# Expert stage of an attention, mixture-of-experts and feed-forward kernel: weight low halves, token order, last narrowing and a branch are rearranged

## The chip, the cores and the metric

The kernel runs on one core of a Trainium2 chip. The metric is device time in microseconds (us) of one execution. Before the change it took 735.32 us (median of 3 runs, 734.01 to 735.62).

## The reference

Three stages, all in float32. Attention over 2 batches, 8 heads, 768 positions of 64 (each position sees 4 sinks and a window of 128). Its output, 1536 tokens of 512, goes through a top-1 mixture of 8 experts, and what comes out through a feed-forward layer with a Mish-like activation:

```
e_idx = argmax(x @ w_gate); gate_w = softmax(x @ w_gate)[e_idx]
eom = sigmoid(x @ w_output_gate)[e_idx]
for e in range(8):                       # expert stage
    h = relu(x[mask_e] @ w1[e]);  ye = h @ w2[e]        # w1: 512x1024, w2: 1024x512
    out[mask_e] = gate_w * eom * ye
h = out @ w_in                           # feed-forward, 512x2048
return (h * tanh(softplus(h))) @ w_out   # 2048x512
```

w_in and w_out arrive as float64 and have to be made into float32 on the chip.

## The kernel before

**Stages.** Attention and routing fill about the first 160 us, the expert stage goes from there to about 470 us, the feed-forward from there to the end. The routing writes each token's row, scaled by its gates, to its expert's place in a table in DRAM and counts the tokens of each expert.

**Split operands.** TensorE multiplies in a reduced format (`fp32r`), so every operand of the expert and feed-forward stages is split into a high half (a rounding copy, on ScalarE) and a low half (value minus high half, an elementwise subtraction). A product is high x high, high x low and low x high. `split_w(unit, p)` (L206, L200) does this for weight piece p: 0 to 3 are four pieces of w1, 4 to 7 of w2, each 128x1024 float32 (512 KB), loaded by SP into one of eight buffers `RAW[p]` by `load_w`/`fetch` (L180, L1037). The low half goes to VectorE for even p and to GpSimd for odd p (L203 to L204). `W1` has two sets of pairs that take turns; `W2S` has one.

**Units and tiles.** The expert with the most tokens left over comes last. A unit is an expert; a tile is 192 of its tokens. Seven units have one tile, the last has three: ten tiles, listed in `TILES`. (A branch `If(more > 0)` at L1132 would run extra tiles if an expert had more tokens; it isn't taken on these inputs: the trace has ten tiles.) The first 128 rows of expert 0 are computed apart, ahead of the tiles, in full float32 (`pre_chunk`, L836): two hidden halves of 512, `first` and `second`, with the weight splits of unit 0 between them. The second hidden half's `second` stands at L1056, then its result is copied to `preT` (L1057), then comes the branch, then `preT` and the first tile's x are transposed.

**One tile** (`tile_mm`, L998) has four blocks b. `first(b)`: 16 matmuls of XS with w1 into PSUM `h`; ScalarE copies the low product, VectorE adds (`t`), ScalarE takes the relu as high half of `hs`, VectorE its low half. `second(b)`: 16 matmuls of `hs` with w2 into `Y`. The order is first 0, 1, 2, second 0, first 3, second 1, then `nxt`, second 2, second 3. `nxt` is `split_x` (L980) of the next tile's x: for each of two halves four transposes on TensorE, a high copy on ScalarE and a subtraction on VectorE into `XS`. `put` (L992) takes `Y` out to `yT`, in the next tile. After each step `tick(i)` issues side work by the tables at L1154 to L1156: weight splits and fetches, steps of the narrowing, and id scatters.

**Order.** Inside `manual_schedule` the named engines run in the order of the program text; each engine works its queue strictly in order, with semaphores between engines. Elsewhere a planner orders the instructions. SP only issues DMAs: a load into `RAW[p]` waits in SP's queue until that buffer's low half has been taken.

**Token order.** `posi` holds each token's place in the sorted order. `place_ids` (L950) scatters token numbers by it into `order` in DRAM, 12 indirect DMAs from GpSimd's queue over the tiles; at the start of the last unit GpSimd loads `idx` back from there (L1176). The output rows are scattered by `idx` at the end.

**Narrowing.** w_in's float64 words become float32 by four operations (`narrow_steps`, L213: a scaling and three integer operations). Sixteen pieces of 128x512; ten are done during attention, the last six (10 to 15) in the tiles (`IN_D`), scaled on GpSimd, stored to `wi32` in DRAM, and loaded back into `RAW` in the last unit (`fetch(E, p)`), where their splits follow.

Of the kernel before, what the change touches and what calls it, by code (L numbers as in the profile page):

```python
# [27 lines left out]
E = 8  # L28
# [15 lines left out]
def tile_kernel(  # L44
# [21 lines left out]
    order = dram.tile([NT, 1], I32, name="order")  # L66
# [71 lines left out]
    tokid = const.tile([P, B * NB], I32, name="tokid")  # L138
# [9 lines left out]
    nc.gpsimd.iota(tokid, [[P, B * NB]], base=0, channel_multiplier=1)  # L148
# [284 lines left out]
    col = mid.tile([P, P], F32, name="col")  # L433
    nc.gpsimd.iota(col, [[1, P]], base=0, channel_multiplier=0, allow_small_or_imprecise_dtypes=True)
# [401 lines left out]
    def pre_chunk():  # L836

        hs = [xpre, rs.tile([P, 512], F32, name="preh1")]
        hT = [rs.tile([P, 512], F32, name="prehT0"), xpre]
# [6 lines left out]
        hps, pts = bank2(), bank2()  # L846
        hps, pts = [hps[:, c] for c in range(2)], [pts[:, c] for c in range(2)]
# [41 lines left out]
    steps = rs.tile([P, E, NX], F32, name="steps")  # L889
# [56 lines left out]
    pre_second, pre_hold = pre_chunk()  # L946
    rt_.close()
    prev = []

    def place_ids(i):  # L950
        sc = nc.gpsimd.indirect_dma_start(
            out=order[:, :], out_offset=bass.IndirectOffsetOnAxis(ap=posi[:, i:i + 1], axis=0),
            in_=tokid[:, i:i + 1], in_offset=None,
        )
        for o in prev:
            tc.declare_no_dep(sc.ins, o.ins, reason="each token has its own place")
        prev.append(sc)

    att.close()


# [5 lines left out]
    nrp = moe.enter_context(tc.tile_pool(name="nrp", bufs=2))  # L967
    hb = moe.enter_context(tc.tile_pool(name="hb", bufs=4))
    tb = moe.enter_context(tc.tile_pool(name="tb", bufs=2))
# [10 lines left out]
    def split_x(xr):  # L980
        pt = bank2()
        for t in range(2):
            for d in range(NP):
                nc.tensor.transpose(pt[:, t, d * HW:(d + 1) * HW], xr[:, t, d * P:(d + 1) * P], ident[0:HW, 0:HW])  # L984
            pv_ = pt[:, t, 0:NP * HW].rearrange("p (d c) -> p d c", c=HW)
            xs_ = XS.rearrange("p d s (c t) -> p d s t c", t=2)
            nc.scalar.activation(xs_[:, :, 0, t], pv_, AF.Copy)
            nc.vector.tensor_tensor(xs_[:, :, 1, t], pv_, xs_[:, :, 0, t].bitcast(F32), ALU.subtract)  # L988
# [9 lines left out]
    def tile_mm(w1s, w2s, nxt, tick):  # L998
# [3 lines left out]
        def first(b):  # L1002
# [13 lines left out]
            nc.vector.tensor_tensor(t, hp[:, :, 0:W], t, ALU.add)  # L1016
            nc.scalar.activation(hs[:, :, 0], t, AF.Relu)  # L1017
# [11 lines left out]
        with tc.manual_schedule(engines=WS):  # L1029
            tick(0)  # L1030
            for i, step in enumerate((
                    lambda: first(0), lambda: first(1), lambda: first(2), lambda: second(0), lambda: first(3),
                    lambda: second(1), nxt, lambda: second(2), lambda: second(3))):
                step()
                tick(i + 1)
# [19 lines left out]
    with tc.manual_schedule(engines={ET.PE}):  # L1055
        pre_second(1, 0, 4)  # L1056
    nc.vector.tensor_copy(preT, yps)  # L1057
    more = values(cnti[0:1, 0:1], mybir.ALL_ENGINES, NX)[0]

    def extra_tiles():  # L1060
# [4 lines left out]
        big3 = [xs_.tile([P, NX, E], F32, name=f"b3{c}") for c in range(2)]  # L1065
        ej, sj, lj, rj = [xs_.tile([P, NX], F32, name=f"j{c}") for c in range(4)]
        j7 = xs_.tile([P, NX], F32, name="j7")
        t64_ = xs_.tile([P, E, E], F32, name="t64_")
        exf = xs_.tile([P, NX, 4], F32, name="exf")
# [57 lines left out]
        for p_ in range(4, 8):  # L1127
            split_w(0, p_)
# [11 lines left out]
    unit_at(1)  # L1140
    for p_ in range(4):
        lw_ = fetch(1, p_)
    with tc.manual_schedule(engines={ET.PE, ET.Activation, ET.DVE}):
        pt_ = bank2()
# [3 lines left out]
        split_x(xr0)  # L1148
    for p_ in range(4, 8):
        fetch(1, p_)  # L1150
# [3 lines left out]
    SPL2 = {0: (0, 1), 1: (2,), 2: (3,)}  # L1154
    SPL1 = {4: (0,), 5: (1,), 6: (2,), 8: (3,)}
    IN_D = {t: (NA + t - 1,) for t in range(1, 7)}  # L1156
    assert NA == 10
    for u in range(NA, NA + 2):
        load_in(u, nrm)
    was = [None]  # L1160
    nst = {}
    for t, (u, k_) in enumerate(TILES):
        if t + 1 < NTL:
            u1, k1 = TILES[t + 1]
            if k1 == 0:
                if u1 + 1 < E:
# [11 lines left out]
        def tick(i):  # L1178
            if i == 1 and was[0] is not None:
                put(was[0])  # L1180
            if u and not k_:
                for p_ in SPL2.get(i, ()):
                    split_w(u, 4 + p_)
                    if u + 1 < E:
                        fetch(u + 1, 4 + p_)
            if u + 1 < E:
                for p_ in SPL1.get(i, ()):
                    split_w(u + 1, p_)
                    fetch(u + 2, p_)
            if u == E - 1:  # L1190
                if k_ == 0 and i == 8:
                    for p_ in range(4, 8):
# [225 lines left out]
```

## Time and profile before

| | |
|---|---|
| median of 3 runs | 735.32 us |
| the profiled execution | 742.38 us |
| its span (first to last instruction) | 740.7 us |
| mean granted TensorE clock | 0.908 of full speed |
| busy: TensorE, VectorE, ScalarE, GpSimd | 633.8, 413.6, 419.0, 203.1 us |

The profile is of one execution. A busy TensorE is not TensorE at its peak: its records include half-clock stretches, and matmuls overlap. In a row, `L984` is the kernel's line, `h<-ident,xr` the tiles written and read, `x4` the number of records put together, and `[8.21 <-DVE XS L988]` says that the engine had been idle for 8.21 us and what ended that. PE is TensorE, DVE VectorE, ACT ScalarE, POOL GpSimd, SP the engine that issues most DMAs. Engines that are off the critical path may idle at no cost.

### The profile page before, as it was taken

Reading aid. Unit: us, or ns where it says so; the run is one execution under the profiler, and the core shown is the slowest. Engines: PE = TensorE matmul, PEld = TensorE weight load, DVE = VectorE, ACT = ScalarE, POOL = GpSimd, SP = SyncE. Lnnn points to the kernel's source line nnn. Section 1 sums busy time; section 2 is a strip of 40 time slices with the busy share of each in tenths; the row PEclk is TensorE's granted clock in tenths of the full one; section 3 lists DMA queues with packets and bytes.
Section 4 is the critical chain, followed back from the end, with each engine's and each line's share of the span. In section 5 each row is a group of like instructions: output and inputs, shape, how many; then the busy total and the mean of one; then the engine's idle time right before and its main releaser. Section 6 shows DMA issues by size and latency. Waiting matters only on the chain.

```text
span 740.7 us, 10023 instructions
## 1 busy us (share of the span) xinstructions
PE 633.8 (86%) x3524; PEld 532.0 (72%) x3524; DVE 413.6 (56%) x847; ACT 419.0 (57%) x769; POOL 203.1 (27%) x175
## 2 busy tenths in 40 slices
PE   6998998677875957859655989899999999999996
PEld 4665666443875956859654989788888888888884
DVE  6797889766337476575571442898763221332122
ACT  4776777425335336254360442797788676776663
POOL 3544447526045363472543111000002000020002
PEclk9899989868788889779796999999999999999999
DMA  7888754414755768788985200333301000010001
GB/s 156 198 224 230 227 184 147 137 69 125 248 188 91 221 141 209 177 181 203 114 223 115 101 1 1 114 120 109 113 1 53 5 1 0 1 58 0 1 0 58
DMA packets 67409, 84.15 MB, mean 114 GB/s; under 512 B 43088, under 2 KB 43088, under 8 KB 67344
## 3 DMA queue, kind: packets, MB, share of 16 engines
q1 hardware_dynamic: 64848, 77.05, 40.6%
q0 software_dynamic: 2352, 6.31, 2.4%
q8 instruction: 31, 0.51, 0.3%
q14 instruction: 34, 0.28, 0.1%
q10 hardware_dynamic: 144, 0.00, 0.0%
HBM read 68.40 MB, written 14.95 MB: 113 GB/s over the span
## 4 chain that ended last, share of the span: by engine, by line
PE 28%; issue 27%; DVE 8%; ACT 5%; DMA 4%; POOL 2%; SPq 0%; POOLq 0%; DVEq 0%; ACTq 0%
PE hp L1273 7%; PE acc L1290 6%; PE Y L1024 5%; PE h L1008 4%; PE h L1011 2%; PE Y L1026 2%; DVE wal L204 2%; DMA order<-tokid,posi 2%; DVE wbl L204 2%; DVE wcl L204 1%; DVE t L1016 1%; ACT wch L202 1%; PE h L984 1%; POOL out_dram L1306 1%; DMA raw<-in_moe_w_dram 1%
## 5 line engine op out<-in xcount | busy, mean ns | idle before, releaser
L1024 PE MATMUL Y<-hs,wch 128*128 128x384 f32 x320 | 110.2, 406 | 0.0
L1324 DVE TENSOR_TENSOR fx<-hp,fx 128x512 f32<-128x512 f32 x48 | 30.9, 685 | 113.4 <-ACT fx L1321 113.4
L1306 POOL DMA_INDIRECT out_dram<-nr,idx x12 | 11.6, 964 | 277.2 <-DVE nr L1302 154.0
L1026 PE MATMUL Y<-hs,wcl 128*128 128x192 f32 x320 | 87.0, 272 | 0.0
L1026 PEld LDWEIGHTS Y<-hs,wcl 128*128 128x128 f32 x320 | 70.4, 220 | 0.0
L1024 PEld LDWEIGHTS Y<-hs,wch 128*128 128x128 f32 x320 | 69.9, 218 | 0.0
L1015 ACT ACTIVATE t<-h 128x384 f32<-128x384 f32 x40 | 19.3, 482 | 88.5 <-PE h L1011 88.5
L1315 ACT ACTIVATE fx<-hp,nln 128x512 f32<-128x512 f32 x48 | 33.1, 690 | 60.1 <-PE hp L1273 59.8
L1016 DVE TENSOR_TENSOR t<-h,t 128x384 f32<-128x384 f32 x40 | 22.1, 553 | 80.3 <-ACT t L1015 80.0
L204 POOL TENSOR_TENSOR wcl<-raw,wch 128x1024 fp32r<-128x1024 f32 x16 | 40.6, 2538 | 85.6 <-ACT wch L202 74.1
L984 PE MATMUL h<-ident,xr 96*128 96x96 f32 x80 | 13.4, 304 | 57.7 <-DVE XS L988 57.6
L568 POOL TENSOR_TENSOR p<-p,sm 128x512 f32<-128x512 f32 (+1 forms) x48 | 46.9, 1005 | 43.7 <-DVE sm L561 24.6
L556 ACT ACTIVATE p<-ms,nm 128x272 f32<-128x272 f32 (+1 forms) x96 | 47.2, 495 | 17.0 <-DVE nm L554 16.4
L984 PEld LDWEIGHTS h<-ident,xr 96*128 96x128 f32 x80 | 9.6, 172 | 59.8 <-DVE XS L988 59.6
L1017 ACT ACTIVATE hs<-t 128x384 fp32r<-128x384 f32 x40 | 21.0, 525 | 43.8 <-DVE t L1016 43.8
L554 DVE CUSTOM_DVE_ANT_0 ms<-s,m 128x272 f32<-128x272 f32 (+1 forms) x96 | 36.5, 407 | 16.2 <-PE s L298 15.9
L1008 PE MATMUL h<-XS,wbh 128*128 128x384 f32 x192 | 44.0, 351 | 0.0
L1018 DVE SCALAR_TENSOR_TENSOR hs<-t,hs 128x384 fp32r<-128x384 f32 x40 | 28.2, 706 | 23.6 <-ACT hs L1017 23.6
L1273 PE MATMUL hp<-yh,wah 128*128 128x512 f32 x96 | 38.3, 399 | 2.1 <-ACT yh L1223 2.1
L1332 DVE TENSOR_TENSOR gl<-fx,gh 128x512 fp32r<-128x512 f32 x48 | 31.5, 689 | 13.6 <-ACT gh L1328 6.2
L222 DVE SCALAR_TENSOR_TENSOR nt<-nr,nt 128x512 int32<-128x512 int32 x32 | 38.7, 1208 | 0.6
L1273 PE MATMUL hp<-yh,wal 128*128 128x512 f32 x96 | 37.9, 395 | 0.0
(275 smaller groups left out, 1749.2 us busy)
## 6 DMA issues: line engine op xcount, KB each, us to landing
raw<-in_moe_w_dram SPq DMA_DIRECT2D x64, 512.0 KB, 6.7
nr<-in_moe_w_in_dram SPq DMA_DIRECT2D x16, 512.0 KB, 6.1
nr<-in_moe_w_out_dram SPq DMA_DIRECT2D x16, 512.0 KB, 3.7
table<-zer SPq DMA_DIRECT2D x17, 256.0 KB, 5.2
wi<-nt SPq DMA_DIRECT2D x16, 256.0 KB, 3.7
raw<-wi SPq DMA_DIRECT2D x8, 512.0 KB, 10.6
xr<-table SPq DMA_DIRECT2D x10, 384.0 KB, 8.1
vr<-in_v_dram SPq DMA_DIRECT2D x16, 192.0 KB, 3.3
```

Of the source, the lines that this page charges most:

```text
L204: eng.tensor_tensor(lo, src, hi.bitcast(F32), ALU.subtract)
L222: lambda: v_.scalar_tensor_tensor(di, hi_, -2147483648, di, ALU.bitwise_and, ALU.bitwise_or),
L554: nc.vector.tensor_tensor_reduce(ms[:, 0:w], s[j][:, 0:w], m, 1.0, 3.0e38, ALU.add, ALU.min, nm[:, j, i:i + 1])
L556: nc.scalar.activation(p[:, j, i, o:o + w], ms[:, 0:w], AF.Exp, bias=nm[:, j, i:i + 1], scale=-1.0, accum_out=sm[:, j, i:i + 1])
L568: nc.gpsimd.tensor_tensor(pb, pb, sm[:, :, i:i + 1].unsqueeze(3).to_broadcast([P, 2, 2 - s0, P]), ALU.mult)
L1008: nc.tensor.matmul(hp[:, f, 0:2 * W], lhsT=w1s[d][0][:, c], rhs=XS[:, d].rearrange("p s c -> p (s c)"), start=(d == 0), stop=False, skip_g ...
L1024: nc.tensor.matmul(Y[:, c, 0:2 * W], lhsT=wh, rhs=hT[b][:, f].rearrange("p s c -> p (s c)"), start=(b == 0 and f == 0), stop=False, skip_g ...
L1026: nc.tensor.matmul(Y[:, c, 0:W], lhsT=wl, rhs=hT[b][:, f, 0], start=False, stop=(b == 3 and f == 1), skip_group_check=True)
L1273: nc.tensor.matmul(h, lhsT=wt[:, (fb % 8) * P:(fb % 8 + 1) * P], rhs=xx[d], start=(k_ == 0), stop=(k_ == 11))
L1290: nc.tensor.matmul(accs[w][tb], lhsT=g_[:, tb * P:(tb + 1) * P], rhs=w_[:, c], start=(fb == 0 and k_ == 0), stop=(fb == NF - 1 and k_ == 2))
L1315: nc.scalar.activation(x_, st[n]["h"], AF.Sigmoid, bias=nln2)
L1332: nc.vector.tensor_tensor(gl, st[n]["x"], st[n]["gh"].bitcast(F32), ALU.subtract)
```

## The change

- Inside the tiles every weight low half goes to VectorE. The ten tiles have 80 steps (`slot`, eight per tile), and a list `jobs` gives each step at most one weight piece: ScalarE takes its high half in that step, VectorE its low half in the next (`low`), and the fetch of the same piece of the next unit is issued right behind.
- `slot` calls stand inside `first` (between the `t` sum and the relu) and at other places of the tile; `split_x` does all eight transposes first, then both high copies, then both subtractions.
- The pieces 10 to 15 of w_in are narrowed on VectorE in the ninth tile, straight into `RAW[5]` to `RAW[7]`; only pieces 8 and 9 and the first half come from `wi32`.
- The id scatters, `order` and its load go. In the ninth tile VectorE makes one-hots of the places, in the tenth TensorE multiplies them (12 small bf16 matmuls) into the ids, which go to `idx`.
- `pre_chunk` is cut in two: the branch `If(more > 0)` stands after the first part; the second part (`rest`) follows it. Fetches of unit 1's first four pieces stand ahead of `rest`. Register values for unit 2 are loaded there too.
- Buffers: `hs` 3 instead of 4, `t` 3 instead of 2; `preh`, `prehT` in a pool of their own.

```diff
@@ pre_chunk @@
             first(1, 0, 2)
-            turn(hT[0], hs[0], pts[0])
+            turn(hT[0], hs[0], bank2()[:, 0])
             for p_ in range(2, 4):
                 split_w(0, p_)
             first(1, 2, 4)
             relu(1)
+
+        def rest():
             second(0, 0, 2)
             split_w(0, 4)
-            hold = turn(hT[1], hs[1], pts[1])
+            turn(hT[1], hs[1], bank2()[:, 0])
             for p_ in range(5, 8):
                 split_w(0, p_)
             second(0, 2, 4)
-        return second, hold
+            second(1, 0, 4)
+
+        return rest
@@ split_x @@
-            nc.scalar.activation(xs_[:, :, 0, t], pv_, AF.Copy)
-            nc.vector.tensor_tensor(xs_[:, :, 1, t], pv_, xs_[:, :, 0, t].bitcast(F32), ALU.subtract)
+        for t in range(2):
+            nc.scalar.activation(xs_[:, :, 0, t], pv_[t], AF.Copy)
+        for t in range(2):
+            nc.vector.tensor_tensor(xs_[:, :, 1, t], pv_[t], xs_[:, :, 0, t].bitcast(F32), ALU.subtract)
@@ tile_mm @@
             nc.vector.tensor_tensor(t, hp[:, :, 0:W], t, ALU.add)
+            slot(i)
             nc.scalar.activation(hs[:, :, 0], t, AF.Relu)
...
         with tc.manual_schedule(engines=WS):
-            tick(0)
...
+            slot(0)
+            first(0, 1)
+            first(1, 2)
+            first(2, 3)
+            second(0)
+            slot(4)
+            first(3, 5)
+            second(1)
+            slot(6)
+            nxt()
+            second(2)
+            slot(7)
+            second(3)
@@ ahead of the tiles @@
     xr0 = load_x(P)
-    with tc.manual_schedule(engines={ET.PE}):
-        pre_second(1, 0, 4)
-    nc.vector.tensor_copy(preT, yps)
     more = values(cnti[0:1, 0:1], mybir.ALL_ENGINES, NX)[0]
...
     unit_at(1)
+    unit_at(2)
     for p_ in range(4):
-        lw_ = fetch(1, p_)
+        fetch(1, p_)
+    with tc.manual_schedule(engines={ET.PE, ET.Activation}):
+        pre_rest()
+    for p_ in range(4, 8):
+        fetch(1, p_)
     with tc.manual_schedule(engines={ET.PE, ET.Activation, ET.DVE}):
+        nc.vector.tensor_copy(preT, yps)
+        split_x(xr0)
...
+    for t, (u, k_) in enumerate(TILES):
+        if u < E - 1:
+            own = [(u, p_) for p_ in (5, 6, 7)] if u else [None] * 3
+            jobs += own + [(u + 1, p_) for p_ in (0, 1, 2, 3, 4)]
+        elif k_ == 0:
+            jobs += [(u, p_) for p_ in (5, 6, 7)] + [(E, p_) for p_ in range(4)] + [None]
+        elif k_ < LT_ - 1:
+            jobs += [("n", x_) for x_ in range(NA, 16)] + [None] * 2
+        else:
+            jobs += [None] * 4 + [(E, p_) for p_ in (4, 6, 5, 7)]
+    def low():
+        while waits:
+            u, p_ = waits.pop(0)
+            hi, lo = wpair(u, p_)
+            nc.vector.tensor_tensor(lo, RAW[p_], hi.bitcast(F32), ALU.subtract)
+            if u + 1 < E or u + 1 == E and p_ <= 4:
+                fetch(u + 1, p_)
+    def job(j):
+        if j is not None and j[0] != "n":
+            nc.scalar.activation(wpair(*j)[0], RAW[j[1]], AF.Copy)
+        low()
+        if j is not None and j[0] == "n":
+            r0, c0 = in_piece(j[1])
+            for x_ in narrow_steps(RAW[4 + r0 // P][:, c0 - 1024:c0 - 512], nrm[j[1] % 2], scale_dve):
+                x_()
+            load_in(j[1] + 2, nrm)
+        elif j is not None:
+            waits.append(j)
+    def hot_of_places():
+        c12 = col[:, 0:NTB]
+        v_.tensor_scalar(pos2[:, 0], posi, P - 1, None, ALU.bitwise_and)
+        v_.tensor_scalar(pos2[:, 1], posi, 7, None, ALU.logical_shift_right)
+        v_.tensor_copy(posf2, pos2)
+        v_.tensor_tensor(hot, col.unsqueeze(1).to_broadcast([P, NTB, P]),
+                         posf2[:, 0].unsqueeze(2).to_broadcast([P, NTB, P]), ALU.is_equal)
...
+    def ids_of_places():
+        ps = bank2()
+        for a in range(NTB):
+            nc.tensor.matmul(ps[:, 0, 0:2 * NTB], lhsT=hot[:, a], rhs=blk[:, a].rearrange("p s m -> p (s m)"),
+                             start=(a == 0), stop=(a == NTB - 1))
+        nc.scalar.activation(ids, ps[:, 0, 0:2 * NTB].rearrange("p (s m) -> p s m", s=2), AF.Copy)
+        v_.scalar_tensor_tensor(ids[:, 0], ids[:, 1], float(P), ids[:, 0], ALU.mult, ALU.add)
+        v_.tensor_copy(idx, ids[:, 0])
@@ loop over the tiles @@
-            nc.gpsimd.dma_start(out=idx, in_=order.rearrange("(i p) o -> p (i o)", p=P))
+            for x_ in range(NA, NA + 2):
+                load_in(x_, nrm)
+        def slot(i):
+            if i == 0 and was[0] is not None:
+                put(was[0])
+            job(jobs[8 * t + i])
+            if t == NTL - 2 and i == 6:
+                hot_of_places()
+        tile_mm(W1[u % 2], W2S, (lambda: split_x(xr1)) if t + 1 < NTL else ids_of_places, slot)
...
     with tc.manual_schedule(engines={ET.Activation, ET.DVE}):
         put(was[0], range(NP + 1))
+        low()
```

## Rows read from the trace of the kernel before

**Rows 1.** The page's busy tenths of TensorE in 40 slices of the span

```profile
PE   6998998677875957859655989899999999999996
```

**Rows 2.** A middle tile on TensorE: start us, us, line, operation, [idle before it <-releaser]

```profile
276.51 0.88 PE L1008 MATMUL h<-XS,wbh 128*128 128x384 f32 x4
...
283.42 0.36 PE L1024 MATMUL Y<-hs,wch 128*128 128x384 f32 x1
...
285.69 0.90 PE L1008 MATMUL h<-XS,wbh 128*128 128x384 f32 x4
...
290.27 0.50 PE L984 MATMUL h<-ident,xr 96*128 96x96 f32 x4
298.98 0.90 PE L984 MATMUL h<-ident,xr 96*128 96x96 f32 x4 [8.21 <-DVE XS L988]
```

**Rows 3.** Waits of all engines from 210 to 390 us: total us, times, longest

```profile
PE h L984 <- DVE XS L988: 53.4, 7, 8.2
```

**Rows 4.** The same tile on VectorE

```profile
283.27 1.23 DVE L204 TENSOR_TENSOR wcl<-raw,wch 128x1024 fp32r<-128x1024 f32 x1 [0.39 <-DMA xr<-table]
...
285.56 0.56 DVE L1018 SCALAR_TENSOR_TENSOR hs<-t,hs 128x384 fp32r<-128x384 f32 x1 [0.59 <-ACT hs L1017]
...
295.43 3.03 DVE L204 TENSOR_TENSOR wal<-raw,wah 128x1024 fp32r<-128x1024 f32 x1 [0.27 <-ACT wah L202]
```

**Rows 5.** The same tile on GpSimd

```profile
294.53 2.85 POOL L204 TENSOR_TENSOR wal<-raw,wah 128x1024 fp32r<-128x1024 f32 x1 [3.13 <-ACT wah L202]
```

**Rows 6.** The same tile on ScalarE

```profile
279.06 0.49 ACT L1015 ACTIVATE t<-h 128x384 f32<-128x384 f32 x1 [6.61 <-PE h L1011]
...
285.43 1.04 ACT L202 ACTIVATE wch<-raw 128x1024 fp32r<-128x1024 f32 x1
```

**Rows 7.** 2 us windows: busy us (xcount) by engine, granted clock, DMA share, GB/s

```profile
186.00:188.00 2.00, 0.90 (x4) 0.61 (x4) 0.47 (x2) 0.51 (x1) 0.00 (x0) 0.50 1.01 391
282.00:284.00 2.00, 2.00 (x18) 2.00 (x16) 1.29 (x2) 1.62 (x3) 0.00 (x0) 1.00 1.00 247
300.00:302.00 2.00, 2.00 (x9) 2.00 (x9) 1.51 (x2) 1.38 (x2) 2.00 (x2) 0.50 0.88 358
```

**Rows 8.** TensorE at the stage's start, first and eighth tile, and feed-forward start

```profile
176.82 3.60 PE L859 MATMUL Y<-raw,xpre 128*128 128x512 f32 x8
...
183.68 0.63 PE L1146 MATMUL h<-ident,preT 128*128 128x128 f32 x4 [3.27 <-DVEq L1132]
...
188.44 1.62 PE L1008 MATMUL h<-XS,wah 128*128 128x384 f32 x4 [1.28 <-DVE XS L988]
...
205.19 0.49 PE L984 MATMUL h<-ident,xr 96*128 96x96 f32 x4
...
405.83 0.53 PE L1011 MATMUL h<-XS,wbl 128*128 128x192 f32 x1 [8.73 <-POOL wbl L204]
...
420.47 0.49 PE L984 MATMUL h<-ident,xr 96*128 96x96 f32 x4
...
470.00 0.50 PE L1273 MATMUL hp<-yh,wah 128*128 128x512 f32 x1 [1.75 <-ACT yh L1223]
```

**Rows 9.** GpSimd beside these stretches

```profile
173.99 2.45 POOL L204 TENSOR_TENSOR wal<-raw,wah 128x1024 fp32r<-128x1024 f32 x1 [2.98 <-ACT wah L202]
176.98 6.05 POOL L204 TENSOR_TENSOR wcl<-raw,wch 128x1024 fp32r<-128x1024 f32 x2 [0.53 <-ACT wch L202]
...
402.31 1.09 POOL L1176 DMA_DIRECT2D idx<-order  x1 [10.16 <-DMA order<-tokid,posi]
```

**Rows 10.** VectorE on 48 elements, and narrowing alone later

```profile
157.07 0.21 DVE L341 TENSOR_TENSOR dl<-L,mx 128x48 f32<-128x48 f32 x1
...
475.18 0.42 DVE L226 TENSOR_SCALAR nt<-nr 128x512 f32<-128x512 f32 x1
...
477.43 0.68 DVE L1264 TENSOR_TENSOR wbl<-nt,wbh 128x512 fp32r<-128x512 f32 x1
```

**Rows 11.** The line that loads w_in pieces: time to landing

```profile
DMA to landing us min/median/max: 4.1/6.1/7.6
```

More of the change, by code (lines that the diff above doesn't have):

```diff
@@ L137, in tile_kernel @@
     ones = mid.tile([P, P], BF16, name="ones")
-    tokid = const.tile([P, B * NB], I32, name="tokid")
+    col = const.tile([P, P], F32, name="col")
+    part = const.tile([P, 1], F32, name="part")
     nc.gpsimd.iota(w8, [[-1, E]], base=E, channel_multiplier=0, allow_small_or_imprecise_dtypes=True)
@@ L147, in tile_kernel @@
     nc.gpsimd.affine_select(upper, ones, [[1, P]], ALU.is_gt, 0.0, base=0, channel_multiplier=-1)
-    nc.gpsimd.iota(tokid, [[P, B * NB]], base=0, channel_multiplier=1)
+    nc.gpsimd.iota(part, [[0, 1]], base=0, channel_multiplier=1, allow_small_or_imprecise_dtypes=True)
+    nc.gpsimd.iota(col, [[1, P]], base=0, channel_multiplier=0, allow_small_or_imprecise_dtypes=True)
     base = [ecap, const.tile([P, E], F32, name="base1")]
@@ L836, in pre_chunk @@
     def pre_chunk():
-        hs = [xpre, rs.tile([P, 512], F32, name="preh1")]
-        hT = [rs.tile([P, 512], F32, name="prehT0"), xpre]
+        hs = [xpre, preh]
+        hT = [prehT, xpre]
         def turn(dst, src, pt):
@@ L844, in turn @@
             return nc.scalar.activation(dst, pt, AF.Copy)
-        hps, pts = bank2(), bank2()
-        hps, pts = [hps[:, c] for c in range(2)], [pts[:, c] for c in range(2)]
+        hps = bank2()
+        hps = [hps[:, c] for c in range(2)]
         def first(hf, a, z):
@@ L945, in tile_kernel @@
     nc.vector.tensor_copy(posi, posf)
-    pre_second, pre_hold = pre_chunk()
     rt_.close()
[L948 to L957, printed above, removed]
     att.close()
+    prp = ExitStack()
+    prp_ = prp.enter_context(tc.tile_pool(name="prp", bufs=1, side="right"))
+    preh, prehT = [prp_.tile([P, DM], F32, name=nm) for nm in ("preh1", "prehT0")]
+    pre_rest = pre_chunk()
     W1[1] = pairs4(ctx.enter_context(tc.tile_pool(name="wp1", bufs=1)), "wb")
@@ L1068, in extra_tiles @@
         t64_ = xs_.tile([P, E, E], F32, name="t64_")
+        big3 = [xs_.tile([P, NX, E], F32, name="b30"), t64_[:, 0:NX]]
         exf = xs_.tile([P, NX, 4], F32, name="exf")
@@ L1147, in tile_kernel @@
         nc.scalar.activation(yT[:, :, 0:P], pt_[:, 0].rearrange("p (d t) -> p d t", t=P), AF.Copy)
-        split_x(xr0)
-    for p_ in range(4, 8):
-        fetch(1, p_)
     TILES = [(u, 0) for u in range(E - 1)] + [(E - 1, k_) for k_ in range(LT_)]
     NTL = len(TILES)
[L1154 to L1159, printed above, removed]
+    jobs = []
@@ new lines, in tile_kernel @@
+    for t, (u, k_) in enumerate(TILES):
[8 more added lines that the diff above has]
+            jobs += [None] * 4 + [(E, p_) for p_ in (4, 6, 5, 7)]
+    assert len(jobs) == 8 * NTL and NA == 10
@@ new lines, in tile_kernel @@
+    jobs.append(None)
+    waits = []
+    def low():
[16 more added lines that the diff above has]
+            waits.append(j)
@@ new lines, in tile_kernel @@
+    hot = xp.tile([P, B * NB, P], BF16, name="hot")
+    blk = xp.tile([P, B * NB, 2, B * NB], BF16, name="blk")
+    pos2 = xp.tile([P, 2, B * NB], I32, name="pos2")
+    posf2 = xp.tile([P, 2, B * NB], F32, name="posf2")
+    ids = xp.tile([P, 2, B * NB], F32, name="ids")
+    NTB = B * NB
+    def hot_of_places():
[5 more added lines that the diff above has]
+                         posf2[:, 0].unsqueeze(2).to_broadcast([P, NTB, P]), ALU.is_equal)
+        v_.tensor_tensor(blk[:, :, 0], c12.unsqueeze(1).to_broadcast([P, NTB, NTB]),
+                         posf2[:, 1].unsqueeze(2).to_broadcast([P, NTB, NTB]), ALU.is_equal)
+        v_.tensor_tensor(blk[:, :, 1], blk[:, :, 0], c12.unsqueeze(2).to_broadcast([P, NTB, NTB]), ALU.mult)
+        v_.tensor_scalar(blk[:, :, 0], blk[:, :, 0], part, None, ALU.mult)
@@ L1165, in tile_kernel @@
             if k1 == 0:
-                if u1 + 1 < E:
+                if u1 + 1 < E and u1 > 1:
                     unit_at(u1 + 1)
```

56 lines of the change are left out of this document (7 added, 49 removed).

## The prediction, made before the changed kernel ran

> **What bounds the kernel now.** I read the page first: in the expert stage TensorE's digits drop again and again, while over the last third, the feed-forward stage, they stay at nine [rows 1]. So the stage that the change touches has slack and the one it leaves alone has none. Then one middle tile on TensorE, which has eight blocks of matmuls and eight transposes to do per tile: after the first four transposes of the next x it stands still for 8.21 us until VectorE has written `XS` [rows 2]. Over the waits between 210 and 390 us that is the largest of TensorE: seven times, 53.4 us [rows 3]. Then the other engines in the same tile. VectorE is late because, just ahead of that subtraction in its queue, a weight low half takes 3.03 us; the same operation takes 1.23 us earlier in the tile [rows 4], in a window in which GpSimd does nothing [rows 7]. The slow one starts at 295.43, and GpSimd's own low half runs from 294.53 to 297.38 [rows 5]: VectorE ends 1.08 us after GpSimd does. So the tile is paced by two engines that hold each other up over low halves, and then by four transposes that wait for the first `XS` subtraction. Once more, in the eighth tile, TensorE waits 8.73 us for a GpSimd low half [rows 8]; that one was queued behind the `idx` load, for which GpSimd had waited 10.16 us until the last id scatter landed [rows 9].
>
> **Lows on VectorE, one per step; transposes together.** TensorE's demand at full clock: four `first` and two `second` blocks, 276.51 to 290.27, 13.76 us; a `second` block is 283.42 to 285.69, 2.27 us, and two are left, 4.54 us; eight transposes, two records of 0.50 us, 1.0 us [rows 2]. Sum 19.3 us. VectorE per tile: eight lows of 1.23, and twelve small operations (four `t` sums, four `hs` lows, two `XS`, two `yT`), all taken at the 0.56 of the `hs` low: 9.84 + 6.72 = 16.6 us [rows 4]. ScalarE: eight high halves of 1.04 and twelve small operations of about 0.5, 14.3 us [rows 6]. Both are under 19.3. In order: a `t` sum stands behind at most one low, so the bank of a block is free about 1.3 us after its matmuls end and wanted again one block (2.29 us) later; the `XS` subtractions end some 1.8 us after the transposes, and two `second` blocks (4.54 us) cover them, now that all eight transposes go first. Three `hs` buffers instead of four suffice: the fourth `hs` is written after `second(0)`. I find no wait of TensorE left over, with about 1 us to spare at the tightest place, the first block's `t` sum behind the two `yT` sums and a low. Weights: SP's queue now holds for each piece a wait for its low and then its fetch, in the order of the lows, and the piece is wanted one tile later, so each has some 17 us. Bytes per tile: eight pieces of 512 KB and 384 KB of x, 4.6 MB in 19.3 us, 238 GB/s; windows with a full DMA share show 247 to 391 GB/s [rows 7]. So a tile costs 19.3 us. From the first tile's transposes to the eighth's are now 420.47 - 205.19 = 215.3 us [rows 8]; seven tiles will take 135.1. Gain 80.2 us, the `idx` wait included, since with the scatters gone GpSimd has nothing queued. The granted clock should stay up too: after its 8 us of idling TensorE is at 0.50 (1.2 GHz) [rows 7]; that loss is part of the 215.3.
>
> The Trainium skill ("SBUF — State Buffer", Who interferes with whom) says that a VectorE operation with two SBUF inputs and a GpSimd operation that reads SBUF lock each other out for a whole instruction, and that DMA never slows an engine. The tile agrees: 297.38 plus one uncontended low gives the end seen. By that rule every low goes to 1.23 us; if DMA writes slowed VectorE, lows would stay at 3.03, which is a rival below.
>
> **The last narrowing, in SBUF.** Six pieces move into tile nine, steps 0 to 5, all four operations of each on VectorE, and their loads start at tile eight, behind its predecessor's fetches on SP. Four operations take 477.43 - 475.18 = 2.25 us where nothing disturbs them [rows 10]; six pieces, 13.5 us. The tile's small operations are 6.7 us. The one-hots of the places: 1536 elements by the slope between 48 (0.21 us [rows 10]) and 1024 (1.23 us [rows 4]), 1.0 ns each, 1.8 us; three operations on 144 at 0.31 and three tiny ones at 0.2, 1.5 us. Sum 23.5 us: here VectorE is the bound. Piece 12 waits for a load issued when piece 10 is done (two buffers); queued behind it on VectorE are the `hs` low and the `t` sum, for which TensorE waits. A load lands 4.1 to 7.6 us after issue [rows 11]; in between VectorE has 3.4 us of work (piece 11 and two block operations). At 4.1, as the weight loads are gone by then, I add 1 us per pair, twice: 25.5 us; at 7.6 it is 31. The fourth `hs` low and the one-hots come late, TensorE waits some 3 us before its last `second` block and again before tile ten, and I charge tile ten 1.6 us of half clock (a middle tile that starts at 298.98 is at 0.50 to at least 302 [rows 2, 7], 3 us or a little more, of which half is lost).
>
> By the Trainium skill ("SBUF — State Buffer", The DMA setup-cost knee) a 512 KB load is estimated at 2 us plus 1.2 us. The row has 4.1 as the least; by the page's figure tile nine would take 24 us. I keep the row.
>
> Tile ten: 19.3 less the transposes' 1.0, plus twelve small bf16 matmuls in their place (0.6; 0.3 to 2), plus 1.6: 20.5 us. Its high halves and lows have steps 4 to 7; the last low stands after the last `yT` sum and delays only low halves of y, which the feed-forward's first eight matmuls cover; without that cover it costs 1.2 us. From tile eight's transposes to the feed-forward: 1.0 + 4.5 + 25.5 + 20.5 + 1.7 (the wait for `yh` [rows 8]) = 53.2 us, now 470.00 - 420.47 = 49.5. Loss 3.7 us. The six stores and three reloads of `wi32` that go were hidden.
>
> **The branch moved up.** Now all engines resume together at 183.68; GpSimd's last low ends at 183.03 [rows 8, 9]. With the branch ahead of the second part of the shared chunk's work (`rest`), only low 3 is before it on GpSimd, which ends at 176.44 [rows 9]; they resume near 177.1. TensorE will have stood since about 173 (176.82 less one hidden half of 3.60 [rows 8] and four transposes), so it starts at half clock. It still has two hidden halves of 3.60 us and four transposes, 7.6 us, then x's transposes and `XS`, 2.6 us: first matmul at 187.3 at full clock, 195 at half, against 188.44 [rows 8]. In return the first tile then runs at full clock: 13.8 us to the transposes instead of 205.19 - 188.44 = 16.75. They come at 201 to 209; I take 205, no change, 4 us either way. SP's fetches of unit 1 start 6 us earlier, behind unit 2's register loads; the piece is wanted 20 us later. The moved `col` and the new `part` are short GpSimd work at the start, beside the first loads: nothing.
>
> **Sum.** 80.2 - 3.7 + 0 = 76.5 us. The profiled execution took 742.4 us (span 740.7), so 665.9; the median shown, 735.3, is 7 us below that execution, and so 658.8. I say 659 us.
>
> **Rivals.** (1) TensorE keeps short waits in each tile: one low (1.23 us) too late at two places, 2.4 us, seven times, gives 676. For it: three engines in tight order with 1 us of slack. Against: the transposes no longer wait for one another. (2) DMA bound: a tile before moved 8 x 512 + 384 + 512 + 256 KB, 5.4 MB, in (215.3 - 8.7) / 7 = 29.5 us, 182 GB/s. If that is the ceiling of this mix, 4.6 MB take 25.2 us, 5.9 more seven times: 700. Against: 391 GB/s at the stage's start [rows 7]. (3) The other side: lows stay long on VectorE although GpSimd is idle, because DMA writes hold it up. At 3.03 us a tile has 8 x 3.03 + 6.7 = 30.9 us of VectorE, seven make 216.6, and with the 3.7 behind them 740; it turns slower from 2.94 us per low. At 3.6 (1.23 plus a wait of 2.4, the length of a GpSimd low [rows 9]) it is 35.5 us per tile, 772. Against: the 1.23 us low ran while the DMA share was 1.00 [rows 4, 7]. (4) It doesn't do what it says: the planner leaves part of the moved work where TensorE waits for it; half the gain, 697.
>
> **Chances.** Forecast 0.76; (1) 0.10; (2) 0.05; (3) 0.02, slower; (4) 0.05; others 0.02, half of them slower. The forecast's own range: tile nine 2 shorter or 6 longer, start 4 either way, tiles 19.0 to 20: 651 to 674. The 8-in-10 range takes in (1): 647 to 679. Faster by over 0.2% (what a measurement of this kernel can tell from no change) 0.96, within it 0.01, slower 0.03.
>
> **What would show it.** Right: eight weight lows per tile on VectorE near 1.23 us, no GpSimd work in the stage, tiles 19 to 20 us apart with the clock at 1.00, one longer tile (24 to 28 us) with VectorE busy throughout, feed-forward starting near 393 us. Wrong: TensorE still waiting for `XS`, lows over 2 us, ScalarE waiting for `raw` to land, or a first tile that starts after 196 us.

## The result, and the profile after

The changed kernel takes 666.3 us (median of 4 runs, 664.71 to 667.05) against 735.47 before (4 runs): 0.906 of the time, interval 0.9032 to 0.9081. The forecast was 659 us, its range 647 to 679. The profiled execution has a span of 665.3 us against 740.7.

TensorE's busy tenths and granted clock, from the page after; the digits of before are in [rows 1].

```profile
PE   6988999877599999999998979999999999999996
...
PEclk9999888968799999999998979999999999999999
```

Counting slices from 1, the dips of the expert stage are gone but for three: slice 11, the branch at its start, and the small ones in slices 22 and 24, tile nine and the stage's end. TensorE's waits in the stage, 205 to 395 us (line, releaser, total, times, longest), answer to [rows 3]:

```profile
PE hp L1309 <- ACT yh L1259: 4.9, 1, 4.9
PE Y L1018 <- DVE hs L1012: 2.8, 2, 2.6
PE h L1001 <- DVE t L1009: 0.5, 1, 0.5
```

All three lie in tile nine or later. The lows on VectorE, 205 to 335 us, grouped by line and shape (count, busy us and mean ns, then idle time before them), against the 1.23 and 3.03 us of [rows 4]:

```profile
L1173 DVE TENSOR_TENSOR wcl<-raw,wch 128x1024 fp32r<-128x1024 f32 x28 | 34.0, 1214 | 0.0
L1173 DVE TENSOR_TENSOR wal<-raw,wah 128x1024 fp32r<-128x1024 f32 x14 | 17.0, 1216 | 0.0
L1173 DVE TENSOR_TENSOR wbl<-raw,wbh 128x1024 fp32r<-128x1024 f32 x13 | 15.8, 1216 | 0.0
```

The stage on TensorE in order of time (start, duration, what it waited for), against [rows 2, 8]:

```profile
175.01 3.75 PE L858 MATMUL Y<-raw,prehT 128*128 128x512 f32 x4 [7.32 <-DVEq L1128]
...
201.44 0.83 PE L975 MATMUL h<-ident,xr 96*128 96x96 f32 x8
...
258.58 0.83 PE L975 MATMUL h<-ident,xr 96*128 96x96 f32 x8
...
334.76 0.83 PE L975 MATMUL h<-ident,xr 96*128 96x96 f32 x8
...
360.68 0.69 PE L1018 MATMUL Y<-hs,wch 128*128 128x384 f32 x1 [2.62 <-DVE hs L1012]
...
365.06 1.53 PE L1001 MATMUL h<-XS,wbh 128*128 128x384 f32 x4
...
389.87 0.79 PE L1309 MATMUL hp<-yh,wah 128*128 128x512 f32 x1 [4.93 <-ACT yh L1259]
```

Read the transposes (L975) as a clock: 201.44, 258.58 three tiles later, 334.76 four more tiles later, 19.05 us a tile throughout. Cutting both executions at the same places: up to the first tile's transposes 205.19 before, 201.44 after (-3.75 us); seven tiles 215.28 and 133.32 (-81.96); from there to the feed-forward 49.53 and 55.11 (+5.58); the feed-forward to the end 270.7 and 275.4 (+4.7). Together -75.4, the difference of the spans. The medians differ by 69.2 only: the profiled execution of before took 742.38 us, and its start was a late one, as the second look below shows.

### The profile page after: what moved, and what is told of

It is laid out like the page before. It is cut to its first block, busy times and chain, and to the rows that moved or that the text cites. A ratio compares the mean times of both kernels' runs of the same rounds, so it can differ in the third digit from the quotient of the medians.

```text
span 665.3 us, 9962 instructions
## 1 busy us (share of the span) xinstructions
PE 614.8 (92%) x3536; PEld 511.9 (77%) x3536; DVE 410.0 (62%) x892; ACT 418.6 (63%) x770; POOL 102.3 (15%) x126
## 4 chain that ended last, share of the span: by engine, by line
PE 41%; issue 26%; DVE 2%; POOL 2%; DMA 1%; ACT 0%; POOLq 0%; ACTq 0%
PE Y L1018 9%; PE hp L1309 8%; PE h L1001 8%; PE acc L1326 6%; PE h L1004 5%; PE Y L1020 4%; DMA nr<-in_moe_w_in_dram 1%; POOL out_dram L1342 1%; POOL wcl L205 1%; PE h L975 1%; DVE raw L222 0%; DVE raw L223 0%; ACT t L988 0%; DVE yT L989 0%; DVE raw L221 0%
## 5 line engine op out<-in xcount | busy, mean ns | idle before, releaser
L1018 PE MATMUL Y<-hs,wch 128*128 128x384 f32 x320 | 96.8, 367 | 2.8 <-DVE hs L1012 2.8
L1020 PE MATMUL Y<-hs,wcl 128*128 128x192 f32 x320 | 81.6, 255 | 0.0
L1018 PEld LDWEIGHTS Y<-hs,wch 128*128 128x128 f32 x320 | 61.2, 191 | 3.2 <-DVE hs L1012 3.2
L1020 PEld LDWEIGHTS Y<-hs,wcl 128*128 128x128 f32 x320 | 62.2, 194 | 0.0
L555 ACT ACTIVATE p<-ms,nm 128x272 f32<-128x272 f32 (+1 forms) x96 | 47.3, 495 | 17.5 <-DVE nm L553 17.4
L1008 ACT ACTIVATE t<-h 128x384 f32<-128x384 f32 x40 | 19.6, 490 | 29.4 <-PE h L1004 29.4
L1326 PE MATMUL acc<-wdh,gh 128*128 128x512 f32 x96 | 37.8, 394 | 0.0
L1326 PE MATMUL acc<-wdl,gh 128*128 128x512 f32 x96 | 37.6, 392 | 0.0
L1173 DVE TENSOR_TENSOR wcl<-raw,wch 128x1024 fp32r<-128x1024 f32 x30 | 36.4, 1214 | 0.0
L988 ACT ACTIVATE t<-Y 128x384 f32<-128x384 f32 (+1 forms) x22 | 10.2, 463 | 39.8 <-PE Y L1020 32.9
L299 PE MATMUL s<-kh,qh 64*128 64x272 f32 (+1 forms) x96 | 24.8, 420 | 9.3 <-DVE nm L553 9.3
L604 ACT ACTIVATE ph<-pt 128x512 f32<-128x512 f32 (+1 forms) x48 | 25.9, 557 | 10.5 <-PE pt L296 10.5
```

The costliest lines, as they stand in the source:

```text
L555: nc.scalar.activation(p[:, j, i, o:o + w], ms[:, 0:w], AF.Exp, bias=nm[:, j, i:i + 1], scale=-1.0, accum_out=sm[:, j, i:i + 1])
L1018: nc.tensor.matmul(Y[:, c, 0:2 * W], lhsT=wh, rhs=hT[b][:, f].rearrange("p s c -> p (s c)"), start=(b == 0 and f == 0), stop=False, skip_g ...
L1020: nc.tensor.matmul(Y[:, c, 0:W], lhsT=wl, rhs=hT[b][:, f, 0], start=False, stop=(b == 3 and f == 1), skip_group_check=True)
L1173: nc.vector.tensor_tensor(lo, RAW[p_], hi.bitcast(F32), ALU.subtract)
L1326: nc.tensor.matmul(accs[w][tb], lhsT=g_[:, tb * P:(tb + 1) * P], rhs=w_[:, c], start=(fb == 0 and k_ == 0), stop=(fb == NF - 1 and k_ == 2))
```

## The experiments

All ran beside the kernel before, whose median was 735.7 to 736.0 us on these chips. Ratios are against that median; the changed kernel's own is 0.9057 (0.9032 to 0.9081). "Seven tiles" is the time from the first tile's transposes to the eighth's. "The chunk" is the work on the first 128 rows of expert 0, ahead of the tiles.

**Odd lows back on GpSimd** (in the changed kernel):

```diff
-            nc.vector.tensor_tensor(lo, RAW[p_], hi.bitcast(F32), ALU.subtract)
+            (nc.gpsimd if p_ % 2 else nc.vector).tensor_tensor(lo, RAW[p_], ...)
```

> The changed kernel, but the low halves of odd pieces go to GpSimd again, one per step. Theory (VectorE and GpSimd hold each other up): VectorE lows that start while GpSimd works take 2 to 3 us again, the t and hs operations slip behind them, and TensorE, which has about 1 us of slack per tile, waits 0.5 to 2.5 us in each of seven tiles: 670 to 685 us. Rival (GpSimd was only slow by itself, and spreading one low per step hides it): lows on VectorE stay at 1.22 us, tiles stay 19.05 us apart, 664 to 669 us.

670.38 us, ratio 0.913 (0.9088 to 0.9172); seven tiles 138.0 us. VectorE and then GpSimd in one tile:

```profile
217.97 1.22 DVE L1173 TENSOR_TENSOR wal<-raw,wah 128x1024 fp32r<-128x1024 f32 x1
221.78 3.43 DVE L1173 TENSOR_TENSOR wal<-raw,wah 128x1024 fp32r<-128x1024 f32 x1
```

```profile
218.49 5.64 POOL L1173 TENSOR_TENSOR wal<-raw,wah 128x1024 fp32r<-128x1024 f32 x2 [3.61 <-ACT wah L1179]
```

The hold-up is there: the low that meets GpSimd's takes 3.43 us instead of 1.22. But it costs only 4.7 us over seven tiles, the low end of what the theory gave: in this order TensorE wants little at once of what stands behind a long low (between 200 and 340 us its longest wait for `XS` is 1.0 us).

**x's halves in turn again** (in the changed kernel): `split_x` as it was, four transposes, copy, subtraction, twice.

```diff
-        for t in range(2):
-            nc.scalar.activation(xs_[:, :, 0, t], pv_[t], AF.Copy)
-        for t in range(2):
-            nc.vector.tensor_tensor(xs_[:, :, 1, t], pv_[t], ...)
+            nc.scalar.activation(xs_[:, :, 0, t], pv_, AF.Copy)
+            nc.vector.tensor_tensor(xs_[:, :, 1, t], pv_, ...)
```

> The changed kernel, but x is turned half by half as before (four transposes, high copy, subtraction, then the next four). Theory: the second four transposes wait for the first subtraction, which stands behind a low in VectorE's queue: about 1.8 us of TensorE per tile, nine times, 16 us: 679 to 686 us, granted clock still 1.00 in the tiles. Rival (with short lows VectorE is early enough, so the order of the transposes carries nothing): 665 to 669 us.

692.84 us, ratio 0.943 (0.9385 to 0.9472), more than the theory's 679 to 686. The second four transposes wait 1.81 us in every tile, as expected, and in tile nine much longer, behind the narrowing:

```profile
205.76 0.55 PE L976 MATMUL h<-ident,xr 96*128 96x96 f32 x4 [1.81 <-DVE XS L979]
...
387.23 0.90 PE L976 MATMUL h<-ident,xr 96*128 96x96 f32 x4 [8.77 <-DVE XS L979]
```

Seven tiles take 150.7 us (+17.4), and tile eight's transposes to the feed-forward 64.1 (+9.0): the two add up to the 26 us. The clock was not 1.00 throughout, as the theory had it: behind two of the seven waits it fell (0.57 from 228 to 230 us), and those tiles took 22.7 us instead of 21.1.

**`rest` ahead of the branch** (in the changed kernel):

```diff
     pre_rest = pre_chunk()
+    with tc.manual_schedule(engines={ET.PE, ET.Activation}):
+        pre_rest()
...
-    with tc.manual_schedule(engines={ET.PE, ET.Activation}):
-        pre_rest()
```

> The changed kernel, but the second part of the shared rows' work stands ahead of the branch again. Theory: TensorE works through instead of standing 7.3 us at 167.7, but stands later, between that work and the first tile, until GpSimd's lows of pieces 5 and 7 end; the first tile starts at about 186 to 189 us as before and runs its first blocks at half clock, 3 us lost: 667 to 673 us. Rival (the move is worth the whole early wait): 673 to 680 us. Rival (the move costs its wait, and undoing it helps): 660 to 664 us.

661.6 us, ratio 0.902 (0.8965 to 0.9079), which the time alone doesn't tell from 0.9057. The chunk's first matmul and the first tile's transposes, in the changed kernel:

```profile
163.56 1.98 PE L850 MATMUL h<-raw,preT 128*128 128x512 f32 x4 [0.53 <-ACT xpre L287]
...
201.44 0.83 PE L975 MATMUL h<-ident,xr 96*128 96x96 f32 x8
```

and with `rest` ahead of the branch:

```profile
162.20 1.98 PE L850 MATMUL h<-raw,preT 128*128 128x512 f32 x4 [0.53 <-ACT xpre L287]
...
177.77 0.85 PE L977 MATMUL h<-ident,xr 96*128 96x96 f32 x8 [1.78 <-SPq L1130]
...
180.95 0.41 PE L1003 MATMUL h<-XS,wah 128*128 128x384 f32 x1 [1.89 <-ACT yT L1150]
...
196.36 0.83 PE L977 MATMUL h<-ident,xr 96*128 96x96 f32 x8
```

The first tile's transposes come 5.1 us earlier, but 1.4 us of this were there before the branch: the chunk itself began earlier, and over all traces it begins anywhere between 159.0 and 167.1 us. Counted from the chunk, the transposes come after 34.2 us instead of 37.9. So moving the branch up cost 3.7 us: with `rest` ahead, TensorE fills the time in which it now stands 7.32 us for the branch. Both theories that called the move a gain fall; the rival that undoing it helps holds.

**All lows on VectorE** (alone, in the kernel before):

```diff
-        eng = eng or (nc.vector if p % 2 == 0 else nc.gpsimd)
+        eng = eng or nc.vector
```

> The kernel before, with all weight low halves on VectorE and nothing else changed (old tables of steps, id scatters and narrowing in place). Theory (the mutual hold-up of VectorE and GpSimd is the largest part of the gain): lows fall to about 1.22 us, tiles go from 29 to 21 to 24 us, the 8.7 us wait in the eighth tile goes as nothing stands behind the idx load: 675 to 700 us. Rival (VectorE becomes the bound, as the lows stand in bunches ahead of the subtraction): tiles stay at 27 to 30 us, 715 to 740 us.

728.15 us, ratio 0.990 (0.9877 to 0.9929). Waits of TensorE, 200 to 425 us, and VectorE ahead of one late `XS`:

```profile
PE h L984 <- DVE XS L988: 46.1, 8, 7.3
```

```profile
267.92 1.23 DVE L204 TENSOR_TENSOR wbl<-raw,wbh 128x1024 fp32r<-128x1024 f32 x1 [0.39 <-ACT wbh L202]
269.06 0.42 DVE L220 TENSOR_SCALAR nt<-nt 128x512 int32<-128x512 int32 x1
...
270.12 1.22 DVE L204 TENSOR_TENSOR wbl<-raw,wbh 128x1024 fp32r<-128x1024 f32 x1
271.26 0.55 DVE L988 TENSOR_TENSOR XS<-h,XS 128x384 fp32r<-128x384 f32 x1
```

Every low is short, and the `XS` wait only falls from 8.2 to 7.3 us. VectorE is now late because the old tables put lows and narrowing steps in a bunch ahead of `XS`. Still the seven tiles fall to 195.8 us, by 19.5. The total hides that, because the edit reaches further than the change: unit 0's lows, ahead of the tiles, go to VectorE too (the change leaves them split), and the first transposes come 46.7 us after the chunk's first matmul instead of 37.1 (second look below).

**The transposes together** (alone, in the kernel before), and then **together with all lows on VectorE**: the new `split_x`; and that with the line above.

> The kernel before with one part of the change alone: the eight transposes of x together, then both copies, then both subtractions; the weight lows stay split between VectorE and GpSimd, in their old places. Theory A (the wait for the first XS is the cost, whoever else is late): 53.4 us of waits go, and the half clock behind them, -50 to -65, 670 to 685 us. Theory B (lows and XS come late as well, and are only waited for in another place, in the next tile's first block): -15 to -35, 700 to 720, and TensorE waits for XS or a low ahead of a first block. Other side: slower, if the two subtractions now stand together behind a long low and the next first block needs both.

> The kernel before with two parts of the change: the transposes together and every low on VectorE; the planner still places the splits, and the id scatters and the idx load stay. If these two parts are all that the seven tiles need: tiles of about 19 us but for tile eight, and about 735 less 73, 660 to 668. If the fixed places (one high half and one low per step, between t and relu) carry a part: 675 to 700, with VectorE and ScalarE working in bunches between the transposes, as they did with the lows alone on VectorE. By e11 and e4 the two would add up if independent.

The first: 716.87 us, ratio 0.974 (0.9712 to 0.9768), seven tiles 201.2. Its waits of TensorE, 205 to 405 us:

```profile
PE h L1013 <- POOL wbl L204: 20.3, 4, 12.3
PE h L1010 <- DVE XS L990: 16.9, 6, 2.9
PE h L1013 <- POOL wal L204: 8.8, 3, 3.3
```

That is theory B: the 8.2 us waits are gone, and TensorE waits in the next tile's first block instead, for `XS` and for a GpSimd low. The second: 688.75 us, ratio 0.936 (0.933 to 0.9392), seven tiles 162.7. Waits, 205 to 395 us:

```profile
PE h L1010 <- DVE XS L990: 13.9, 6, 2.3
PE Y L1026 <- DVE hs L1020: 3.0, 6, 1.0
PE h L984 <- DMA xr<-table: 2.1, 1, 2.1
```

The same edit to the lows lengthens the start here too. The first transposes come 49.1 us after the chunk; TensorE's wait at the branch is, here and then in the second look at the kernel before:

```profile
PE h L1148 <- DVEq L1134: 13.6, 1, 13.6
```

```profile
PE h L1146 <- DVEq L1132: 4.4, 1, 4.4
```

GpSimd, rid of its lows, now runs six id scatters ahead of that branch (163.10 to 173.89 us); whether they are what it waits for isn't shown.

In the tiles, this is what follows a wait for `XS` (2 us windows: busy us by engine, granted clock, DMA share, GB/s):

```profile
331.00:333.00 2.00, 1.29 (x4) 1.32 (x5) 2.00 (x4) 0.00 (x0) 0.00 (x0) 0.71 0.97 324
333.00:335.00 2.00, 2.00 (x9) 2.00 (x9) 1.43 (x2) 0.00 (x0) 0.00 (x0) 0.50 0.99 286
```

A wait of 2.3 us for `XS` is paid almost twice: the matmuls behind it run at 0.50 for some 3.4 us (331.7 to 335.1), of which half is lost. Lined up, the seven tiles take 215.3 us; 195.8 with the lows moved; 201.2 with the transposes together; 162.7 with both; 133.3 with the fixed places as well. No part carries the gain alone: the two together save 52.6 us where each alone saves 19.5 and 14.1, and the last 29.4 come with the rest of the rewritten order (one high half and one low per step, the low between the `t` sum and relu, the narrowing and the id scatters out of these tiles). How these share the 29.4 us was not tested. In the wait shown, ScalarE's copies of x already start late, at 328.97, behind three high halves, while the transposes stand at 323.37; the two narrowing steps ahead of VectorE's subtraction take 1.1 us.

**The idx load at the last tile** (in the kernel before):

```diff
-        if t == E - 1:
+        if t == NTL - 1:
             nc.gpsimd.dma_start(out=idx, ...)
```

> The kernel before, with the idx load issued at the last tile instead of ahead of tile eight, so that GpSimd doesn't stand before it while the id scatters land; the scatters stay. Theory (the 8.73 us wait of TensorE in tile eight is all that the scatters cost): the wait goes, GpSimd's low halves of that tile are ready on time, -8 to -11 us with the half clock behind it, about 726. Rival (the scatters themselves delay GpSimd's lows in other places): more than 12 us can't come from this edit alone, and the wait only moves to the last tile: 733 to 736.

735.84 us, ratio 0.999 (0.9962 to 1.0018), and no finding on the load: the planner put it in the same place, and all instructions of GpSimd and SP stand in the order of before. What the id scatters cost was therefore not measured. The run is a second look at the kernel before:

```profile
161.99 1.98 PE L851 MATMUL h<-raw,preT 128*128 128x512 f32 x4 [0.53 <-ACT xpre L286]
...
199.10 0.49 PE L984 MATMUL h<-ident,xr 96*128 96x96 f32 x4
```

Seven tiles take 213.6 us, then 47.9 and 270.3. The profiled execution of before had thus come to its tiles some 6 us late: its chunk began at 167.09, 5.1 us later than here, and its first four matmuls took 3.78 us instead of 1.98. Counted from the chunk, the first transposes come after 37.1 us here and 38.1 there, against 37.9 in the changed kernel: the start as a whole is within 1 us of what it was, where the spans alone showed 3.75 us gained. The seven tiles' saving is 80 to 82 us by either.

**32 bytes more among the constants** (in the changed kernel):

```diff
-    part = const.tile([P, 1], F32, name="part")
+    part = const.tile([P, 16], F32, name="part")[:, 0:1]
```

> The changed kernel with 32 bytes more in its constants, so that the weights, XS and the hidden buffers stand in SBUF where they stood before the change (224 instead of 192 modulo 512 bytes); nothing else differs. Theory (place of the matmul operands): the feed-forward's groups of 12 matmuls of 512 columns go from 2.80 and 2.76 us back to 2.72, the stage from 275.4 to about 271 us, the total to about 661.5 us (-4.7). Rival (the 4.7 us come from something else, such as the state in which the stage begins, or from one execution to the next): groups stay at 2.76 to 2.80, total at 666 within 1.

660.95 us, ratio 0.897 (0.8952 to 0.8997). Matmuls of the feed-forward, 475 to 735 us, by line (count, busy us, mean ns), first the changed kernel and then with the 32 bytes:

```profile
L1309 PE MATMUL hp<-yh,wah 128*128 128x512 f32 x60 | 23.7, 396 | 0.0
...
L1309 PE MATMUL hp<-yh,wch 128*128 128x512 f32 x32 | 12.7, 398 | 0.0
```

```profile
L1309 PE MATMUL hp<-yh,wah 128*128 128x512 f32 x60 | 23.3, 389 | 0.0
...
L1309 PE MATMUL hp<-yh,wch 128*128 128x512 f32 x32 | 12.5, 389 | 0.0
```

The mean falls from 396 to 398 ns to 389, and the starts of successive matmuls stand 0.227 us apart instead of 0.233 at the same clock of 1.00. The feed-forward takes 270.1 us instead of 275.4. All seven traces with the changed kernel's places show 275.2 to 275.8 us in this stage, the seven others 269.8 to 271.1. The two programs differ only in where the later buffers lie, so their place costs 5.3 us; that it acts on the matmuls is shown by their own spacing. The seven tiles take 133.3 us in both, so it is these matmuls of 512 columns that feel it. Which buffers matter, and how they must lie, is open.

**The last low half ahead of the last `yT` sums** (in the changed kernel):

```diff
             job(jobs[8 * t + i])
+            if t == NTL - 1 and i == 7:
+                low()
```

> The changed kernel with the last weight low half one slot earlier in the last tile, ahead of its yT sums instead of behind them. Theory (the high halves of y are queued behind that low as well): the wait of TensorE at the feed-forward's start falls from 4.93 us to about 1.7, and the half clock after it is shorter: -3 to -5 us, about 662. Rival of my prediction's sort (the low is hidden behind the first eight matmuls of the feed-forward): no change, 666 within 1. Other side: the low one slot earlier holds up the fourth hs of the last tile, TensorE waits there instead, and the total stays or grows by up to 1 us.

664.88 us, ratio 0.9025 (0.8995 to 0.9055), which the time alone doesn't tell from 0.9057. The profile does. VectorE and ScalarE of the changed kernel, where all high halves of y stand behind the low:

```profile
387.66 0.36 DVE L989 TENSOR_TENSOR yT<-Y,t 128x192 f32 x1 [0.40 <-ACT t L988]
387.93 1.22 DVE L1173 TENSOR_TENSOR wbl<-raw,wbh 128x1024 fp32r<-128x1024 f32 x1
```

```profile
389.18 2.20 ACT L1259 ACTIVATE yh<-yT 128x512 fp32r<-128x512 f32 x4 [1.56 <-DVE wbl L1173]
```

and with the low moved, ScalarE and TensorE:

```profile
387.39 0.62 ACT L1261 ACTIVATE yh<-yT 128x512 fp32r<-128x512 f32 x1
```

```profile
388.07 0.50 PE L1311 MATMUL hp<-yh,wah 128*128 128x512 f32 x1 [1.75 <-ACT yh L1261]
```

The copies of y alternate with the sums again, the wait is 1.75 us, and from tile eight's transposes to the feed-forward it takes 51.8 us instead of 55.1. So the copies waited for that low. Why they did is read from the kernel only: `yh` takes the memory that `RAW` gives up, and the low still reads `RAW`.

**The one-hots in tile ten** (in the changed kernel):

```diff
-            if t == NTL - 2 and i == 6:
+            if t == NTL - 1 and i == 4:
```

> The changed kernel with the one-hots of the places built on VectorE in tile ten, slot 4, instead of in tile nine, slot 6. Theory (tile nine is bound by VectorE): tile nine falls from 24.4 to about 21.2 us and tile ten, where VectorE has slack, stays: -3 to -4.5 us, about 662.5. Rival (tile nine is paced by the landing of the pieces of w_in): no change, 666 within 1, and TensorE's wait stands in the same place under another name. Other side: in tile ten the one-hots (1.8 us in one operation) hold up the t sum of the fourth block and add up to 2 us there.

668.09 us, ratio 0.9065 (0.904 to 0.909): no change, and from tile eight's transposes to the feed-forward 55.2 us as before. TensorE still waits for the fourth `hs` low:

```profile
359.93 0.69 PE L1018 MATMUL Y<-hs,wch 128*128 128x384 f32 x1 [3.08 <-DVE hs L1012]
```

The theory falls in part, and so does the rival, since no load paces the tile (VectorE waits 0.5 us for loads in all). VectorE bounds tile nine up to that low, which stands ahead of the one-hots; the one-hots and `XS` behind it end beside the last `second` block (360.68 to 365.06 in the changed kernel, at half clock), so they were hidden.

**The hidden half in a buffer of its own** (in the changed kernel):

```diff
-        hT = [prehT, xpre]
+        hT = [zer, xpre]
```

> The changed kernel with the transposed hidden half of the shared chunk in a buffer that was free all along, instead of in the attention's memory that the scatters of the table read from. Theory (ScalarE's copy of those four transposes waits for the scatters to land): the copy goes from 169.21 to about 165.9 us, the branch resumes about 3.3 us earlier, total about -3, 663. Rival (the branch is held by GpSimd's third low half at 174.2 anyway): no change at the branch, 666 within 1.

666.49 us, ratio 0.9053 (0.9028 to 0.9077): no change. ScalarE's copy does go from 169.21 to 165.59, and GpSimd's third low ends 3.7 us earlier, yet ScalarE resumes behind the branch at nearly the same time (174.98 before this edit):

```profile
174.27 1.06 ACT L203 ACTIVATE wch<-raw 128x1024 fp32r<-128x1024 f32 x1 [4.20 <-DVEq L1128]
```

```profile
168.16 2.34 POOL L205 TENSOR_TENSOR wal<-raw,wah 128x1024 fp32r<-128x1024 f32 x1 [0.43 <-ACT wah L203]
```

The rival's number holds and its reason doesn't: that low ends at 170.50, and VectorE's last one ahead of the branch at 171.58. What holds the branch for the 2.7 us after that is open.

**Three together**: `rest` ahead of the branch, the 32 bytes, the last low half early.

> The changed kernel with three edits together, each run alone before: rest ahead of the branch, the 32 bytes more in the constants, the last low half ahead of the last yT sums. If they are independent, each keeps what its own stage showed: start -5.1 us (first tile's transposes 196.4 against 201.4), feed-forward -5.3 (270.1 against 275.4), last tile -3.2 (from tile eight's transposes to the feed-forward 51.9 against 55.1). Total 666.3 less 13.6, about 653 us (650 to 656). Rival (they share a cause, such as the half clock at the feed-forward's start): less than the sum, 655 to 659.

655.11 us (653.40 to 655.62), ratio 0.889 (0.8872 to 0.8917), the fastest of all. First transposes at 198.05, seven tiles 133.4, then 52.0 and 269.8 us: the gains of the last tile and of the feed-forward stay whole. The chunk began at 163.50, so the start takes 34.6 us from there and keeps 3.3 of the branch's 3.7 us. The three thus add up; of the 13.6 us expected, 1.4 were the earlier chunk of the branch run.

## Why the prediction was right, and where a term was off

- **Seven tiles at 19.3 us, TensorE-bound: right.** 19.05, no wait, clock 1.00, 133.3 us against 135.1. ScalarE and VectorE kept their slack, and x's subtractions are covered by two `second` blocks as worked out.
- **The cause named for before: only part of it.** The prediction put the tile down to two engines that hold each other up, then to transposes that wait for the first `XS`. The hold-up is real (3.43 against 1.22 us), but taking it away alone saved 19.5 of the 82 us in the seven tiles and left 7.3 of the 8.2 us of a wait. Both named causes taken away together saved 52.6. The rest is the order: what stands ahead of `XS` in the queues of VectorE and ScalarE. The sum didn't notice, since it took the whole new order at once.
- **Tile nine 25.5 us: right** (340.02 to 365.06, 25.0), paced by VectorE up to the last narrowed piece. Loads landed in 3.7 us, and VectorE waited for them 0.5 us in all; 1 us per pair was put down. The estimate of 3.2 us by the Trainium skill ("SBUF — State Buffer", The DMA setup-cost knee) gave 24 us for the tile, the 4.1 us of [rows 11] gave 25.5; the measured 3.7 lies between them. The second wait foreseen, before tile ten, didn't come: the one-hots fit beside the last `second` block.
- **Tile ten 20.5 us: right** (365.06 to 384.94, 19.9).
- **The step that failed: the last low half "delays only low halves of y".** It delayed the high halves too: ScalarE's copies began at 389.18, when it had ended. The wait is 4.93 us where 1.7 was put down: 3.2 us, which its experiment gave back.
- **Start: "no change" came out, not for the reason given.** First matmul at 187.61 (187.3 to 195 was given), transposes at 201.44 (201 to 209). Counted from the chunk they come after 37.9 us, against 38.1 and 37.1 before. But the branch's move isn't neutral: it costs 3.7 us, and other parts of the new start, which no run separates, give about 3 back.
- **Feed-forward unchanged: wrong by 4.7 us.** It was put at nothing since its instructions are the same; but their buffers had moved, and undoing 32 bytes of that gave 5.3 us back.
- **659 against 666.3: these two terms are most of the difference.** 3.2 us for the last low and 5.3 for the feed-forward make 8.5; the seven tiles came 1.8 us better than forecast, so 6.7 of the 7.3 us are explained. Taking 7 us off for the median was right, since they belonged to the late start of the profiled execution. Without that the forecast was 665.9, and the changed kernel's profiled execution took 667.05; that this is nearer is luck: the 205 us forecast for the first transposes copied the late start, they came 3.6 us earlier, and that hid most of the feed-forward's 4.7.

Of the rivals, short waits in each tile, long lows and half the gain are excluded by the rows above, and the DMA ceiling of 182 GB/s by 233 to 254 GB/s between 210 and 240 us, at a clock of 1.00.

## What to carry to other kernels

Before blaming a slow instruction, ask what is queued ahead of the one that is waited for: in the seven tiles shorter lows alone saved 19.5 us, the transposes together alone 14.1, both 52.6, and with the whole new order 82. A wait that is removed from one place shows up at the next in-order queue until the whole order fits, and a wait can bring a stretch of half clock with it: one of 2.3 us did here, waits of 1.8 us did in two tiles of seven. Compare the stages of two executions from the same instruction on, not from the start of the span: here the chunk began up to 8 us apart. When a stage whose code did not change runs slower, look at where its buffers lie.

## What the runs showed of the hardware that was not expected

A matmul of 512 columns took 389 ns or 396 to 398 ns in the same program at the same granted clock, with starts 0.227 or 0.233 us apart, depending only on a shift of 32 bytes in the buffers behind the constants: 5 us in a stage of 270. The hold-up was expected, but not how little it costs where the order leaves slack: a VectorE low took 3.43 us beside two GpSimd lows of 5.64 us together, 1.22 us alone, with DMA moving 195 to 254 GB/s between 210 and 240 us in either kernel, and the seven tiles grew by 4.7 us only.
